# Gated attention and SwiGLU on one core: where the setup work, one chunk's input loads, the pair loads and several side streams are put in the order of the program

## The chip, the core and the metric

The kernel runs on one core of one Trainium2 chip. Its engines are TensorE (PE for matmuls, PEld for weight loads), VectorE (DVE), ScalarE (ACT), GpSimd (POOL) and SyncE (SP); transfers are issued by SP, ACT or POOL and run on the core's 16 DMA engines. The metric is the device time of one execution in microseconds, as the median of the runs; less is better. Times of instructions come from one execution that the hardware profiler recorded.

## What is computed

A sequence of 2048 rows of 640 numbers (`x`) goes through two branches, and a gate per row mixes them:

```python
def _A_ref(x, wq, wk, wv, wo, beta):        # 32 heads of 20, 4 chunks of 512 rows
    q, k, v = ...                            # x @ wq, x @ wk, x @ wv, by heads and chunks
    phi = lambda t: jnp.where(t > 0, t + 1.0, jnp.exp(t))
    g = _sigmoid(beta).reshape(1, H, 1, 1)
    for s in range(N):
        logits = jnp.einsum("bhqd,bhkd->bhqk", qs, ks) * scale + mask
        a_dot = jnp.einsum("bhqk,bhkd->bhqd", _softmax(logits), vs)
        num = jnp.einsum("bhld,bhde->bhle", phi(qs), M)
        den = jnp.einsum("bhld,bhd->bhl", phi(qs), z)[..., None] + 1e-6
        outs.append(g * num / den + (1.0 - g) * a_dot)
        M = M + jnp.einsum("bhld,bhle->bhde", phi(ks), vs)
        z = z + jnp.einsum("bhld->bhd", phi(ks))
    return o @ wo
...
g = _sigmoid((x * gate_w).sum(-1, keepdims=True))
a = _A_ref(x, wq, wk, wv, wo, beta)
b = (_silu(x @ w1) * (x @ w3)) @ w2
return g * a + (1 - g) * b
```

## The kernel before

**Number format.** Nearly every operand of a matmul is split into a high part of reduced precision and the rest (`split`, L204: ACT copies the high part, then DVE or POOL subtracts it), and a product takes three matmuls (`PASSES`: high by high, high by low, low by high).

**Halves.** Most matmuls use 64 of the 128 rows of the array, and the two row halves run side by side. A piece of dense work (`Work`) fills one PSUM bank: its first half is issued, then a no-op on SP that waits for the half's end (L308), and the second half waits for that no-op (L311). So SP's queue carries, beside the loads of weights and the stores, a no-op for each such piece.

**Two streams.** `attention()` (L1812) counts slots. Forty slots are a quad of four heads. In a quad `S_AT` and `T_AT` say at which slot the score matmuls (`s`), for the row maxima, and the transposed ones (`t`), which ACT turns into P by an exponential, are put into a queue; `PV` is the slot of the matmuls of P with V (`o`, line 1651). Two heads (a pair) lie in one of `NST` = 4 tiles `qk`, which `load_pair` (L1522) fills from memory by two DMAs on POOL's queue, at slots 28 and 39 of the quad before. A constant row of -1 stands in the tiles. Beside attention a list of segments (from L2024) brings the dense work: V, Q and K projections, the feed-forward products (`g`, `u` and, for chunks 0 and 1, the shared form `c1 w2 c6 c7 z5 c4 z3` of `ffn_pair`), the down projections (`f`), the reading and writing of the memory (`nd`, `pm`), the normalization (`rr`, `gt`) and the output projection (`op`). The head (L2038 and L2045) comes before attention begins; `LEAD` is the number of slots before the first quad.

**The planner.** The order of all instructions is written by the program itself. Each engine has a planned clock; `later` puts a step behind a planned time, `stages` chains evacuations, `go` adds a duration. `braid(a, b, every, skip)` yields the work of `a` and, each `every` ns of planned matmul time after the first `skip` ns, one step of `b`. Nothing of these times reaches the chip: there, an engine runs its instructions in the written order and waits for what they need. `AGE` (a weight load's least age), `SOON` (when a buffer of raw weights counts as free) and `AHEAD` (how far the second row half may run before the first when no bank is free) are such planned times.

**Around the change.** The setup has three parts: `constants` (L81, with the tile `one` that fills the -1 rows), `gates` (L93, five small DMAs of `beta` on POOL) and `selection` (L111, POOL work on three scratch tiles). Before the change `constants` is called behind the head's first job and `gates` and `selection` behind its second (L2080), ahead of the V tiles. `load_raw(2)` (L731) issues five DMAs of the third chunk's X on SP, all at once, into a buffer (`big_tile`) that the output projection of chunk 0 used before; in the program it stands behind that projection (L2054). `parts` (L813) evacuates a Q or K block through a tile of the ring `hT` (three tiles). `after_3` and `after_4` (L1408, L1419) are evacuations in `ffn_pair`.

Of the kernel before, what the change touches and what calls it, by code (L numbers as in the profile page):

```python
# [20 lines left out]
P = 128  # L21
# [10 lines left out]
RH, LEAD = 3 * DH, 23  # L32
NP, AGE, TS, PV = 2, 3000, 0, 2
LAG = 5
LATE = 4
EARLY = range(2, 6)
# [5 lines left out]
SOON = 700  # L42
COL, COL4, MIN_MM, APART, ISSUE, AHEAD = 0.4533, 1.7, 62, 5, 580, 1500
STEP, READ = 700, 222
EVAC = 3000
KSKIP, QSKIP = 6, 0
# [5 lines left out]
def gated_mix(ctx: ExitStack, tc: tile.TileContext, xT, wqk, wv, w13, w2, w2h, wo, beta, out):  # L52
# [28 lines left out]
    def constants():  # L81
        make_identity(nc, ident)
        nc.gpsimd.memset(mask, 0.0)
        nc.gpsimd.affine_select(mask[:, 384:], mask[:, 384:], pattern=[[-1, P]], base=0,
                                channel_multiplier=1, compare_op=ALU.is_ge, fill=BIG)
        for v in vg:
            nc.gpsimd.memset(v[:, :, VG:], 0.0)
        one = cp.tile([P, KB, L], F32, tag="oall", name="one", bufs=1)[:, 0]
        nc.gpsimd.memset(one, -1.0)
        for i in range(NST):  # L90
            nc.gpsimd.tensor_copy(qk[i][:, 1], one)

# [18 lines left out]
    def selection(base, h0, n, f0, f1):  # L111
# [16 lines left out]
        def done():  # L128
            for a in range(3):
                let(f"sel{base}_{a}")  # L130
            if not base:
# [5 lines left out]
               done=done)  # L137

# [592 lines left out]
    def load_raw(c):  # L731

        wide = big_tile(f"xr{c}")
        xraw[c] = [wide[:, kb * L:(kb + 1) * L] for kb in range(KB)]
        for kb in range(KB):
            store_later(xraw[c][kb], xT[c, :, kb, :], ("x", c, kb))
        return
        yield

    def new_x(c):  # L740

        got = []
        if c not in xraw:
            xraw[c] = []
# [68 lines left out]
    def parts(name, ps, bank, stored, phi=None, done=None, over=None):  # L813

        v = "dve" if over is None else "both"
        s = ht_tile([P, 2, L], FR, name)
# [507 lines left out]
    def ffn_pair(cs, plan, fill):  # L1324
# [4 lines left out]
        def block(j, idx):  # L1329
# [78 lines left out]
            def after_3(ps, bank):  # L1408
                t = H2[0][:, 0]
                stages(bank, ("dve", 690, lambda: nc.vector.tensor_add(ps, f["b"], ps)),  # L1410
                       ("dve", 690, lambda: nc.vector.tensor_mul(t, t, ps), True), done=lambda: end(0, "b"))
# [7 lines left out]
            def after_4(ps, bank):  # L1419
                t = H2[0][:, 1]  # L1420
                stages(bank, ("act", 600, lambda: nc.scalar.activation(t, ps, AF.Tanh, scale=0.5)),
# [390 lines left out]
    def attention():  # L1812


        for m in range(-1, NQUAD + 2):
            for n in range(40):
# [13 lines left out]
                if n in ((22, 32) if m < 0 else (28, 39)) and m + 1 < NQUAD:  # L1830
                    p = 2 * (m + 1) + (n > 28)
                    flush(lambda: all(q % NST != p % NST for _, _, q, _ in units))
                    load_pair(p)
# [200 lines left out]
    for n in range(9):  # L2034
# [10 lines left out]
    head += [braid(braid(chain([v0, v1, (0, islice(up[1], 2)), half, (0, islice(up[1], 15))]), (0, store_sums(A, True)), 1300), (0, load_sums(A)), 1200)]  # L2045
    seg = [braid(up, job_read(1), 4400, 14000)]
# [7 lines left out]
    seg = [braid(chain([d0, d1]), o1, 500, 6000), o2, (0, load_raw(2)), braid(chain([d1b, d2]), xs, 3000, 24400, False)]  # L2054
    seg += [braid(braid(chain([q2, v2]), out0, 900), xs, 1500, 5000)]
    ks = jobs_k_held(B)
    seg += ks[:KSKIP] + [alternate(chain(ks[KSKIP:]), job_plain(B, [0]))]
    segs.append((2 * H + 7, seg))
# [3 lines left out]
    seg += [braid(chain(q[:QSKIP] + [alternate(chain(q[QSKIP:]), job_plain(B, [1]))]), r, 2600, 3000, False)]  # L2062
# [4 lines left out]
    seg = [braid(braid(chain(main), chain([r, job_read(3)]), 1800, 7000), o1, 600, 1000),  # L2067
           braid(chain([o2, job_plain(B, range(4, 8))]), (0, store(1)), 900)]
    segs.append((3 * H + LAG + 5, seg))
    ups = [job_plain(B, range(8, 11)), job_half(3), job_half(2), job_plain(B, range(11, NF))]  # L2070
# [7 lines left out]
    tail = [braid(chain([d1b, d2]), o1, 300, 9000), o2]  # L2078

    def at_job(n):  # L2080
        if n == 0:
            constants()
        elif n == 1:
            gates()
            selection(0, 0, R1H + 1, 0, R1B * P)
# [92 lines left out]
```

## Time and profile before

| | |
|---|---|
| median of 3 runs | 1074.7 us (1073.06 to 1074.82) |
| profiled execution | 1080.68 us |
| its span, first to last instruction | 1079.0 us |
| mean granted clock of TensorE | 0.996 |
| memory traffic | 116.03 MB read, 70.25 MB written |

The span is what the page's lines share out; the profiled execution's own time lies 1.7 us above it. "PE L305" is a helper's line: nearly every dense matmul is issued there, so groups are told apart by the names of their tiles. A bracket in the timeline is the idle time of the engine just before a row, with what ended it.

### The profile page before, as it was taken

Reading aid. Unit: us, or ns where it says so; the run is one execution under the profiler, and the core shown is the slowest. Engines: PE = TensorE matmul, PEld = TensorE weight load, DVE = VectorE, ACT = ScalarE, POOL = GpSimd, SP = SyncE. Lnnn points to the kernel's source line nnn. Section 1 sums busy time; section 2 is a strip of 40 time slices with the busy share of each in tenths; the row PEclk is TensorE's granted clock in tenths of the full one; section 3 lists DMA queues with packets and bytes.
Section 4 is the critical chain, followed back from the end, with each engine's and each line's share of the span. In section 5 each row is a group of like instructions: output and inputs, shape, how many; then the busy total and the mean of one; then the engine's idle time right before and its main releaser. Section 6 shows DMA issues by size and latency. Waiting matters only on the chain.

```text
span 1079.0 us, 29746 instructions
## 1 busy us (share of the span) xinstructions
PE 1059.0 (98%) x11477; PEld 947.7 (88%) x11477; DVE 668.9 (62%) x1892; ACT 534.3 (50%) x1098; POOL 506.8 (47%) x740
## 2 busy tenths in 40 slices
PE   8999999999999999999999999999999999999998
PEld 6999988888889999899887887898788888999998
DVE  7556777777776676565454576765456666554552
ACT  6357565555554654465654544543434443664320
POOL 5213565655644462448454535545645544443230
PEclk9999999999999999999999999999999999999999
DMA  9655765454465755657686859554746455553631
GB/s 312 212 186 200 249 214 154 130 153 126 126 168 138 222 158 145 201 134 239 200 275 199 231 182 294 160 161 131 211 114 182 122 144 144 143 157 116 213 119 50
DMA packets 127109, 189.20 MB, mean 175 GB/s; under 512 B 21196, under 2 KB 65144, under 8 KB 126968
## 3 DMA queue, kind: packets, MB, share of 16 engines
q1 hardware_dynamic: 95928, 132.74, 39.6%
q0 software_dynamic: 23264, 40.40, 15.6%
q10 hardware_dynamic: 7776, 14.16, 3.7%
q8 instruction: 91, 1.49, 0.6%
q14 instruction: 50, 0.41, 0.1%
HBM read 116.03 MB, written 70.25 MB: 173 GB/s over the span
## 4 chain that ended last, share of the span: by engine, by line
PE 91%; DMA 4%; issue 1%; ACT 1%; POOL 1%; DVE 1%; SPq 0%; ACTq 0%; DVEq 0%; POOLq 0%
PE f L305 18%; PE c L305 11%; PE g L305 9%; PE u L305 7%; PE o L1651 7%; PE op L305 7%; PE v L305 6%; PE z L305 5%; PE s L1556 4%; PE t L1618 4%; PE k L305 3%; PE w L305 3%; PE q L305 3%; DMA qk<-qkd 2%; PE pm L305 1%; PE nd L305 1%
## 5 line engine op out<-in xcount | busy, mean ns | idle before, releaser
L1567 DVE CUSTOM_DVE_ANT_0 junk<-s,mask 128x128 bf16<-128x128 f32 (+3 forms) x512 | 251.0, 490 | 132.9 <-PE s L1556 91.3
L209 POOL TENSOR_TENSOR W<-wr,W 128x640 fp32r<-128x640 f32 (+2 forms) x112 | 175.4, 1572 | 149.1 <-ACT W L214 134.0
L1625 ACT ACTIVATE P<-t 128x384 f32<-128x384 f32 (+1 forms) x384 | 181.0, 526 | 126.6 <-PE t L1618 111.2
L305 PE MATMUL g<-X,W 64*128 64x512 f32 x900 | 217.1, 395 | 1.8 <-SPq L308 1.8
L305 PE MATMUL u<-X,W 64*128 64x512 f32 x780 | 191.8, 394 | 0.0
L1634 POOL TENSOR_SCALAR_AFFINE_SELECT P<-P 128x256 f32<-128x256 f32 (+1 forms) x192 | 96.2, 510 | 201.5 <-ACT P L1625 167.8
L214 ACT CAST W<-wr 128x640 fp32r<-128x640 f32 (+2 forms) x189 | 133.8, 720 | 57.9 <-PE f L305 32.5
L305 PE MATMUL f<-XW,W 64*128 64x320 f32 x1536 | 158.9, 310 | 2.6 <-SPq L308 2.6
L305 PEld LDWEIGHTS g<-X,W 64*128 64x128 f32 x900 | 149.0, 185 | 11.0 <-SPq L308 2.7
L305 PEld LDWEIGHTS f<-XW,W 64*128 64x128 f32 x1536 | 151.6, 187 | 4.1 <-SPq L308 3.1
L305 PE MATMUL c<-X,W 64*128 64x512 f32 x612 | 146.7, 396 | 0.1
L305 PE MATMUL f<-W,W 64*128 64x320 f32 x1056 | 137.4, 309 | 0.0
L305 PEld LDWEIGHTS u<-X,W 64*128 64x128 f32 x780 | 130.7, 185 | 5.9 <-issue 0.6
L305 PEld LDWEIGHTS f<-W,W 64*128 64x128 f32 x1056 | 116.3, 186 | 1.1 <-issue 0.8
L305 PE MATMUL c<-S,W 64*128 64x512 f32 x408 | 115.9, 395 | 0.0
L305 PE MATMUL op<-W,oT 64*128 64x320 f32 x960 | 103.7, 307 | 0.0
L305 PEld LDWEIGHTS c<-X,W 64*128 64x128 f32 x612 | 97.8, 185 | 6.2 <-ACT d L1358 0.6
L1577 POOL DMA_DIRECT2D qk<-mr x128 | 73.0, 572 | 63.0 <-DVE mr L1593 55.6
L1556 PE MATMUL s<-qk 60*128 60x256 f32 (+2 forms) x512 | 96.6, 329 | 3.5 <-DMA qk<-qkd 3.4
L305 PEld LDWEIGHTS op<-W,oT 64*128 64x128 f32 x960 | 98.6, 185 | 0.7 <-issue 0.6
L1618 PE MATMUL t<-qk 62*128 62x256 f32 (+2 forms) x512 | 93.7, 327 | 2.7 <-ACT P L1625 1.2
L305 PE MATMUL v<-W,X 64*128 64x320 f32 (+2 forms) x948 | 92.6, 310 | 0.0
(194 smaller groups left out, 2132.5 us busy)
## 6 DMA issues: line engine op xcount, KB each, us to landing
qk<-qkd POOLq DMA_DIRECT2D x128, 240.0 KB, 4.4
wr<-in_w_dram SPq DMA_DIRECT2D x82, 320.0 KB
hd<-H SPq DMA_DIRECT2D x26, 512.0 KB
qkd<-qs SPq DMA_DIRECT2D x20, 512.0 KB
qkd<-ks SPq DMA_DIRECT2D x20, 512.0 KB
wr<-hd SPq DMA_DIRECT2D x32, 320.0 KB
od<-oq ACTq DMA_DIRECT2D x32, 256.0 KB
wr<-in_wo_dram SPq DMA_DIRECT2D x20, 320.0 KB
```

What stands on the lines that cost most here:

```text
L209: return lambda: e.tensor_sub(dst[:, 1], src, dst[:, 0].bitcast(F32))
L214: stages(bank, ("act", ns, lambda: nc.scalar.copy(dst[:, 0], src)), low, done=done)
L305: ins = nc.tensor.matmul(o, l, x, start=not w.more and i == 0 and (r == 0 or not w.todo[0]), stop=i == len(todo) - 1 and (r == 1 or not w. ...
L1556: nc.tensor.matmul(ps[i][:, o:o + n], q[:, qb * P:(qb + 1) * P], k[:, :n], start=qb != 1, stop=qb != 0, skip_group_check=True)
L1567: nc.vector.tensor_tensor_reduce(out=junk[:, :n], in0=ps[i][:, o:o + n], in1=mask[:, L - n:], scale=1.0, scalar=-3.0e38, op0=ALU.add, op1= ...
L1577: nc.gpsimd.dma_start(dst, src)
L1618: nc.tensor.matmul(ps[i][:, o:o + L - q0], k[:, kb * P:(kb + 1) * P], q[:, q0:], start=kb != 2, stop=kb != 3, skip_group_check=True)
L1625: nc.scalar.activation(u["P"][:, i, o:o + n], ps[i][:, b:b + n], AF.Exp, scale=SCALE)
L1634: nc.gpsimd.affine_select(d, d, pattern=[[0, 2], [0, n], [1, P]], base=0, channel_multiplier=-1, compare_op=ALU.is_ge, fill=0.0)
L1651: nc.tensor.matmul(ps[32 * i:32 * i + 32, kb * P:], heads[2 * p + i]["v"][:, kb], pairs[p + i // 2]["P"][:, i % 2, o:o + n], start=kb == 0 ...
```

## The change

- `one` becomes a scratch tile; it fills only three of the four `qk` tiles at once. The new `set_up` calls `gates` and `selection` and fills the fourth tile's row 9000 ns of planned time later. The head calls it behind the first two V tiles (`islice(v0[1], 2)`); `at_job` keeps `constants` alone.
- The Q block `qs1_1` is evacuated through that fourth `qk` tile and not through the ring `hT`.
- `load_raw(2)` waits until the output projection of chunk 0 is planned as done and then yields after each of its five loads; it is a side stream of the down projection (`braid(..., (0, load_raw(2)), 1200, 0)`). `new_x` waits for it.
- The first pair load of a quad is at slot 27 in place of 28. `PV`, `LEAD`, `AGE`, `SOON`, `AHEAD` and `KSKIP` change.
- In `after_4` (`SOFT` holds 2, not 1) the bank is read once less: the multiply by `f["d"]` comes last, from memory to memory, on DVE or POOL. The new branch in `after_3` isn't taken.
- The steps of eight side streams and the ends of two segments change, and one plain tile goes from one segment to the one before.

```diff
-RH, LEAD = 3 * DH, 23
-NP, AGE, TS, PV = 2, 3000, 0, 2
+RH, LEAD = 3 * DH, 22
+NP, AGE, TS, PV = 2, 2500, 0, 3
+SOFT = (0, 2)
-SOON = 700
-COL, COL4, MIN_MM, APART, ISSUE, AHEAD = 0.4533, 1.7, 62, 5, 580, 1500
+SOON = 400
+COL, COL4, MIN_MM, APART, ISSUE, AHEAD = 0.4533, 1.7, 62, 5, 580, 3000
-KSKIP, QSKIP = 6, 0
+KSKIP, QSKIP = 4, 0
...
-        one = cp.tile([P, KB, L], F32, tag="oall", name="one", bufs=1)[:, 0]
+        one = f_tile("one", "pool")
         nc.gpsimd.memset(one, -1.0)
-        for i in range(NST):
+        for i in range(NST - 1):
             nc.gpsimd.tensor_copy(qk[i][:, 1], one)
+        big["one"] = one
...
+    def set_up():
+        gates()
+        selection(0, 0, R1H + 1, 0, R1B * P)
+        def fill():
+            nc.gpsimd.tensor_copy(qk[NST - 1][:, 1], big.pop("one"))
+            let("one", go("pool", 640))
+        later(now() + 9000, fill)
+        return
+        yield
...
     def load_raw(c):
+        while not all((c - 2, qb) in op_done for qb in range(4)):
+            yield 1
         wide = big_tile(f"xr{c}")
         xraw[c] = [wide[:, kb * L:(kb + 1) * L] for kb in range(KB)]
         for kb in range(KB):
             store_later(xraw[c][kb], xT[c, :, kb, :], ("x", c, kb))
-        return
-        yield
+            yield 1
     def new_x(c):
         got = []
+        while c == B[0] and c not in xraw:
+            yield 1
...
-        s = ht_tile([P, 2, L], FR, name)
+        if name == "qs1_1":
+            s = qk[NST - 1]
+            holds[name] = [0.0], 0
+        else:
+            s = ht_tile([P, 2, L], FR, name)
...
             def after_4(ps, bank):
                 t = H2[0][:, 1]
+                if 2 in SOFT:
+                    stages(bank, ("act", 600, lambda: nc.scalar.activation(t, ps, AF.Tanh, scale=0.5)),
+                           ("dve", 690, lambda: nc.vector.scalar_tensor_tensor(t, t, 1.0, ps, op0=ALU.add, op1=ALU.mult), True),
+                           either(690, 1290, lambda v: v.tensor_mul(t, t, f["d"])), done=lambda: end(1, "d"))
+                    return
...
-                if n in ((22, 32) if m < 0 else (28, 39)) and m + 1 < NQUAD:
-                    p = 2 * (m + 1) + (n > 28)
+                if n in ((22, 32) if m < 0 else (27, 39)) and m + 1 < NQUAD:
+                    p = 2 * (m + 1) + (n > 30)
...
-    head += [braid(braid(chain([v0, v1, (0, islice(up[1], 2)), half, (0, islice(up[1], 15))]), (0, store_sums(A, True)), 1300), (0, load_sums(A)), 1200)]
-    seg = [braid(up, job_read(1), 4400, 14000)]
+    head += [braid(braid(chain([(0, islice(v0[1], 2)), (0, set_up()), v0, v1, (0, islice(up[1], 2)), half, (0, islice(up[1], 15))]), (0, store_sums(A, True)), 1300), (0, load_sums(A)), 1800)]
+    seg = [braid(up, job_read(1), 3500, 14000)]
...
-    seg = [braid(chain([d0, d1]), o1, 500, 6000), o2, (0, load_raw(2)), braid(chain([d1b, d2]), xs, 3000, 24400, False)]
-    seg += [braid(braid(chain([q2, v2]), out0, 900), xs, 1500, 5000)]
+    seg = [braid(chain([d0, d1]), o1, 300, 7000), o2, braid(braid(chain([d1b, d2]), (0, load_raw(2)), 1200, 0), xs, 2700, 25400, False)]
+    seg += [braid(braid(chain([q2, v2]), out0, 300), xs, 1500, 3000)]
...
-    segs.append((2 * H + 7, seg))
+    segs.append((2 * H + 6, seg))
...
-    seg += [braid(chain(q[:QSKIP] + [alternate(chain(q[QSKIP:]), job_plain(B, [1]))]), r, 2600, 3000, False)]
+    seg += [braid(chain(q[:QSKIP] + [alternate(chain(q[QSKIP:]), job_plain(B, [1]))]), r, 2300, 0, False)]
...
-    seg = [braid(braid(chain(main), chain([r, job_read(3)]), 1800, 7000), o1, 600, 1000),
-           braid(chain([o2, job_plain(B, range(4, 8))]), (0, store(1)), 900)]
-    segs.append((3 * H + LAG + 5, seg))
-    ups = [job_plain(B, range(8, 11)), job_half(3), job_half(2), job_plain(B, range(11, NF))]
+    seg = [braid(braid(chain(main), chain([r, job_read(3)]), 900, 8000), o1, 1200, 8000),
+           braid(chain([o2, job_plain(B, range(4, 9))]), (0, store(1)), 1200)]
+    segs.append((3 * H + LAG + 6, seg))
+    ups = [job_plain(B, range(9, 11)), job_half(3), job_half(2), job_plain(B, range(11, NF))]
...
-    tail = [braid(chain([d1b, d2]), o1, 300, 9000), o2]
+    tail = [braid(chain([d1b, d2]), o1, 2700, 12000), o2]
...
     def at_job(n):
         if n == 0:
             constants()
-        elif n == 1:
-            gates()
-            selection(0, 0, R1H + 1, 0, R1B * P)
```

More of the change, by code (lines that the diff above doesn't have):

```diff
@@ L1409, in after_3 @@
                 t = H2[0][:, 0]
+                if 1 in SOFT:
+                    u = f["b"]
+                    stages(bank, ("dve", 690, lambda: nc.vector.tensor_add(u, u, ps), True),
+                           either(690, 1290, lambda v: v.tensor_mul(t, t, u)), done=lambda: end(0, "b"))
+                    return
                 stages(bank, ("dve", 690, lambda: nc.vector.tensor_add(ps, f["b"], ps)),
@@ L1420, in after_4 @@
                 t = H2[0][:, 1]
+                if 2 in SOFT:
+                    stages(bank, ("act", 600, lambda: nc.scalar.activation(t, ps, AF.Tanh, scale=0.5)),
+                           ("dve", 690, lambda: nc.vector.scalar_tensor_tensor(t, t, 1.0, ps, op0=ALU.add, op1=ALU.mult), True),
+                           either(690, 1290, lambda v: v.tensor_mul(t, t, f["d"])), done=lambda: end(1, "d"))
+                    return
                 stages(bank, ("act", 600, lambda: nc.scalar.activation(t, ps, AF.Tanh, scale=0.5)),
```

## The prediction

> **What bounds the kernel now.** I read the page's first part, then the chain, then every piece of PE idle time in order of time.
>
> ```profile
> span 1079.0 us, 29746 instructions
> PE 1059.0 (98%) x11477; PEld 947.7 (88%) x11477; DVE 668.9 (62%) x1892; ACT 534.3 (50%) x1098; POOL 506.8 (47%) x740
> PE 91%; DMA 4%; issue 1%; ACT 1%; POOL 1%; DVE 1%; SPq 0%; ACTq 0%; DVEq 0%; POOLq 0%
> ```
>
> PE is busy for 98% of the span and 91% of the chain. The edits leave the matmuls as they are; they move other instructions against them. So the change is worth what it does to the places where PE stops. The timeline of PE shows them as idle time in brackets; these are all the pieces over 0.15 us between its first and last matmul:
>
> ```profile
> 12.35 11.61 PE L904 MATMUL q<-X,W 128*128 128x512 f32 x42 [2.27 <-ACT X L689]
> ...
> 138.91 0.35 PE L1556 MATMUL s<-qk 60*128 60x256 f32 x1 [0.69 <-DMA qk<-qkd]
> 139.94 0.47 PE L1556 MATMUL s<-qk 60*128 60x256 f32 x3 [0.67 <-DMA qk<-qkd]
> ...
> 435.04 0.89 PE L305 MATMUL f<-XW,W 64*128 64x320 f32 x7 [2.57 <-SPq L308]
> ...
> 516.52 0.47 PE L1618 MATMUL t<-qk 62*128 62x256 f32 x3 [0.45 <-DVE m L1567]
> 569.38 0.50 PE L305 MATMUL g<-X,W 64*128 64x512 f32 x1 [1.47 <-SPq L308]
> 610.64 0.50 PE L305 MATMUL g<-X,W 64*128 64x512 f32 x1 [0.37 <-SPq L308]
> ...
> 661.86 0.24 PE L303 MATMUL gt<-ident,gm 64*128 64x64 f32 x1 [1.53 <-DMA gm<-gd]
> 674.24 0.49 PE L1618 MATMUL t<-qk 62*128 62x512 f32 x1 [0.97 <-ACT gate L993]
> 679.10 0.50 PE L1618 MATMUL t<-qk 62*128 62x256 f32 x3 [1.18 <-ACT P L1625]
> ...
> 775.62 0.47 PE L1556 MATMUL s<-qk 60*128 60x256 f32 x3 [0.90 <-DMA qk<-qkd]
> 799.85 0.39 PE L1556 MATMUL s<-qk 60*128 60x256 f32 x2 [0.72 <-DMA qk<-qkd]
> 874.36 0.47 PE L1556 MATMUL s<-qk 60*128 60x256 f32 x3 [0.46 <-DMA qk<-qkd]
> ```
>
> They sum to 14.25 us; the first and the one at 435 make 4.84 of it, the other eleven 9.41. Two cost more than they last. The view by windows gives the granted clock in its third column from the end:
>
> ```profile
> 12.40:15.90 3.50, 3.50 (x9) 2.73 (x10) 3.38 (x6) 3.18 (x6) 0.00 (x0) 0.51 1.05 395
> 426.00:432.00 6.00, 6.00 (x83) 5.99 (x81) 3.41 (x10) 1.79 (x4) 2.09 (x4) 1.00 0.33 85
> 432.50:435.00 2.50, 0.00 (x0) 0.00 (x0) 2.50 (x5) 0.96 (x4) 0.00 (x0) 1.00 0.61 187
> 435.00:439.20 4.20, 4.16 (x34) 4.16 (x36) 0.20 (x1) 1.48 (x3) 0.00 (x0) 0.59 0.94 304
> ```
>
> After the gap of 2.27 us the clock stands at 0.51 for 3.5 us, after that of 2.57 us at 0.59 for 4.2 us: 3.5 x 0.49 = 1.7 us and 4.2 x 0.41 = 1.7 us are lost on top. (34 matmuls in 4.2 us against 83 in 6.0 us say the same.) After the gaps of 1.47 and 1.53 us I see no such stretch. So what can be won is 14.25 + 3.4 = 17.7 us at most.
>
> **The change, part by part.**
>
> *The third chunk's X by pieces (saves 4.2).* SP's rows before the gap at 435:
>
> ```profile
> 432.36 1.28 SPq L802 DMA_DIRECT2D xr<-in_xT_dram  x3
> ...
> 434.32 1.09 SPq L802 DMA_DIRECT2D xr<-in_xT_dram  x2
> ```
>
> SP works through its instructions one behind the other, as the rows show. The five loads write the buffer that the output projection of chunk 0 reads until about 432, and only then can they issue. Behind them stands the no-op of line 308, for which the second row half of an f tile waits, and PE with it. After the change a load is issued only when all four blocks of that projection are planned as done, and one per 1200 ns of planned matmul time, so each holds SP for some 0.4 us (1.28 / 3) and its no-ops pass between. Nothing needs the pieces soon: the splits begin 25400 ns of matmul time into the stage. Gone: 2.57 + 1.7 = 4.3; I leave 0.1 for five short holds. Bounds: 0 (a piece waits as the five did) to 4.3.
>
> *Gates and selection behind V tiles (saves 2.5).*
>
> ```profile
> 4.76 0.91 SPq L684 DMA_DIRECT2D xr<-in_xT_dram  x2
> 5.38 0.73 POOL L94 DMA_DIRECT2D gH<-in_beta_dram  x1
> 6.10 2.09 POOL L96 DMA_DIRECT2D cR<-in_beta_dram  x4
> 11.68 1.14 ACT L689 CAST X<-xr 128x512 fp32r<-128x512 f32 x2 [3.28 <-DMA xr<-in_xT_dram]
> 19.88 0.38 POOL L965 MEMSET V<- 128x128 f32 x1 [10.50 <-DVE W L209]
> q0 software_dynamic: 76, 0.02, 20.3%
> ```
>
> The last X pieces are issued at 4.76 and are waited for until 11.68. Between, POOL issues five small loads; the last row is the DMA view of 8.0 to 11.7, where POOL's queue takes 20.3% of the engines, 0.203 x 3.7 = 0.75 us of each, for 0.02 MB. The five now stand behind the V tile's memset on POOL, at 19.9 or later, when PE has V tiles to work on and no gap before 138; selection follows them on POOL, ends some 3 us later than now, and its first reader is far off. If X comes 0.75 sooner, the gap is 1.5 us, as long as those that leave the clock alone: 0.8 + 1.7 = 2.5. Bounds: 0 (other traffic delays X) to 2.27 + 1.7 = 4.0 (X beats the last matmul at 10.1).
>
> By the Trainium skill ("DMA: Bandwidth & Descriptors", Queues, rings and completion order) each DMA engine serves its queue rows in turn, a packet at a time. By that rule the small loads share engines with X though another queue issues them, and the term is not nothing; by issue order alone it would be 0.
>
> *Pair loads a slot sooner (saves 1.6).*
>
> ```profile
> 767.83 1.58 POOL L209 TENSOR_TENSOR W<-wr,W 128x640 fp32r<-128x640 f32 x1 [2.72 <-ACT W L214]
> 769.34 1.11 POOL L1531 DMA_DIRECT2D qk<-qkd  x2
> POOL qk L1531 <- PE t L1618: 5.9, 4, 4.7
> 777.00 2.29 PE o L1651 x32
> 900.38 2.29 PE o L1651 x32
> ```
>
> Five quads (o to o) take 123.4 us, a slot of 40 therefore 0.62 us. The five gaps of s on qk<-qkd total 3.44; at 138 the two belong to one pair. Moved by 0.62 they save 4 x 0.62, less 0.16 because the last is only 0.46: 2.3. But a weight split of 1.58 us stands right ahead of the load, and the load keeps that place if the split isn't passed. I take 1.6; bounds 0 and 3.44. Sooner also means that POOL may wait for the t matmuls that still read the buffer (5.9 us in four waits now, 0.62 more in each), with masks queued behind; P masks have one slot more (PV 3), so I cost that at nothing here and in the new waits below.
>
> *Reads and output tiles of chunk 1 re-paced (saves 1.8).*
>
> ```profile
> 653.88 0.81 POOL L1744 DMA_DIRECT2D gm<-gd  x1
> 655.00:660.00 5.00, 5.00 (x69) 4.54 (x59) 3.48 (x8) 2.61 (x5) 3.26 (x5) 1.00 1.05 354
> 565.88 2.59 SPq L802 DMA_DIRECT2D qkd<-ks  x2
> ```
>
> The gaps at 661, 673 and 678 (3.68 together) lie where gm is fetched while the DMA engines are full (1.05 of their time). The memory read now starts 3000 ns sooner and steps by 2300 in place of 2600, the normalization begins at 8000 in place of 1000 and steps by 1200 in place of 600, which leaves each fetch twice the time. Half of 3.68: 1.8; bounds 0 and 3.68.
>
> *K and Q stages (saves 0.4).* The gaps at 516, 569 and 610 sum to 2.29. The long one follows 2.59 us in which SP waits to store a K block; KSKIP 4 moves the plain tiles two K blocks forward, so the meeting is another one, better or worse. Bounds -2.29 and 2.29.
>
> *Edits that I cost at nothing.*
>
> ```profile
> L1422 DVE TENSOR_TENSOR c<-d,c x13: 686/693/697, 158.7 to 351.6; 128x512 f32<-128x512 f32 x13
> L303 PE MATMUL gt<-ident,gm x40: 213/222/224, 1026.6 to 1034.3; 64*128 64x64 f32 x40
> 1057.05 17.88 PE L305 MATMUL op<-W,oT 64*128 64x320 f32 x217
> ```
>
> SOFT frees a bank one DVE multiply (693 ns, 13 times) sooner and may send the multiply to POOL; between 140 and 432 PE has no gap, so nothing is won. The Q block in attention's tile and the -1 rows filled later lie under the dense V tiles. In the tail the steps of the last normalization grow from 300 to 2700 ns: ten tiles from about 1021 end near 1021 + 27 = 1048, and the projection starts at 1057; 9 us of cover. Were it gone, PE would wait by the difference.
>
> *New waits (cost 4.3).* SOON, AGE, AHEAD, segment ends and steps shift nearly every queue from 430 to 900. There the trace shows no such order, so I bound it: 0 new waits, or as many as the eleven now, 9.4. A mean of 9.41 / 11 = 0.86; I take five, 4.3, the middle.
>
> **Sum.** 4.2 + 2.5 + 1.6 + 1.8 + 0.4 = 10.5 saved, 4.3 spent: 6.2. The profiled execution took 1080.68 us (span 1079.0 and 1.7 around it), so 1074.5; it is 6.0 above the median of 1074.7. The gaps are absolute, so I take 6.2 from the median: **1068.5 us**. Its own range: the gates' term by its bounds moves it by -1.5 to +2.5, the new waits, taken halfway to their bounds, by -2.2 to +2.5: 1064.8 to 1073.5. Chance 0.56.
>
> **Rivals.**
> - *All goes to its upper end.* 4.2 + 4.0 + 2.3 + 3.7 + 2.3 = 16.5, less 4.3: 12.2, 1062.5. For it: each wait has its edit. Against: POOL's order. 0.12.
> - *Gaps come back elsewhere.* As many new waits as the eleven, 9.4: 10.5 - 9.4 = 1.1, 1073.6. For it: nearly all lie within 2 us, the size by which edits move things. 0.10.
> - *The load isn't spread.* If the planner runs ahead of the chip, the first piece still waits for its buffer: 6.2 - 4.2 = 2.0, 1072.7. Against: SP would have to reach it before the f tile behind the projection. 0.06.
> - *SP blocks PE more (slower).* With SOON 400 a weight load is issued 300 ns sooner after a split that POOL or DVE may not have ended; SP then stands before its no-ops as at 432. A stop like that costs 2.57 + 1.7 = 4.3. The place is the f and g tiles from 430 on. Two of them give 8.6 - 6.2 = +2.4, 1077.1; from the second on it decides. Against: SP's stops reach PE only three times now. 0.12.
> - *The clock isn't lost to gaps of this size.* If the half clock came from elsewhere, 1.7 + 1.7 fall out: 6.2 - 3.4 = 2.8, 1071.9. The two stretches begin right after the two longest gaps, which speaks against it. 0.04. The Trainium skill ("TensorE: Matmul & The Clock Gate", HAM oscillation) gives as the abstract rule that idle gaps over about 3.4 us are to be avoided; by it 2.57 would be harmless, and this trace disagrees with its 0.59.
>
> **Chances.** A measurement tells about 0.2%, 2.1 us, from no change. Of the forecast's 0.56 the end above 1072.6 (0.04) counts as no change. Faster: 0.52 + 0.12 + 0.04 = 0.68. Same: 0.10 + 0.06 + 0.04 = 0.20. Slower: 0.12. The range runs from 1061.5, a microsecond past the best case, to 1077.2, two stops of SP.
>
> **What would show it.** Right: no gap and full clock near 435; the first gap at most 1.5 us and the clock not at half after 12; gaps of s under 0.3; none at 660 to 680. Wrong: L308 ahead of new gaps of 2 us or more, or idle PE before 1057 in the tail. New gaps of together over 10.5 us would turn the sign.

## The result and the profile after

| | before | after |
|---|---|---|
| median | 1074.7 us (1073.06 to 1077.22, 5 runs) | 1062.61 us (1061.73 to 1063.17, 5 runs) |
| ratio of the times, 95% interval | | 0.9885 [0.987, 0.99] |
| profiled execution, its span | 1080.68 us, 1079.0 us | 1063.17 us, 1061.5 us |
| mean granted clock | 0.996 | 1.000 |

The change saves 12.1 us; 6.2 were forecast. The first lines of the page after:

```profile
span 1061.5 us, 29740 instructions
PE 1051.9 (99%) x11477; PEld 939.8 (89%) x11477; DVE 672.4 (63%) x1903; ACT 533.3 (50%) x1098; POOL 499.9 (47%) x729
```

The matmuls are the same 11477. PE's time without work, span less busy time, fell from 20.0 to 9.6 us. The timeline of PE after the change, all pieces of idle time over 0.15 us between its first and last matmul (start, duration, operation, in brackets the idle time just before it and what ended it):

```profile
28.25 2.03 PE L320 MATMUL v<-W,X 64*128 64x320 f32 x24 [0.30 <-SPq L323]
...
129.95 0.39 PE L320 MATMUL pm<-V,pkn 64*128 64x147 f32 x1 [0.71 <-ACT pkn L1060]
...
155.08 0.34 PE L320 MATMUL nd<-Ms,pq 64*128 64x84 f32 x1 [1.02 <-ACT P L1657]
...
160.88 0.50 PE L320 MATMUL w<-X,W 64*128 64x512 f32 x1 [0.31 <-SPq L323]
...
232.06 0.50 PE L320 MATMUL c<-X,W 64*128 64x512 f32 x1 [0.34 <-ACT d L1380]
...
433.26 1.00 PE L320 MATMUL f<-XW,W 64*128 64x320 f32 x10 [0.35 <-SPq L323]
...
688.17 0.44 PE L1650 MATMUL t<-qk 62*128 62x384 f32 x1 [0.57 <-ACT P L1657]
...
799.08 0.49 PE L320 MATMUL g<-X,W 64*128 64x512 f32 x1 [0.95 <-SPq L323]
```

Eight pieces, 4.55 us, in place of thirteen, 14.25 us. Only the place at 433 had a gap before, and there 0.35 is left of 2.57. No row is ended by a DMA any more, where before s on qk<-qkd and gt on gm<-gd were. The windows of after that answer to those shown of before:

```profile
12.00:15.90 3.90, 3.90 (x19) 3.13 (x18) 3.90 (x7) 3.75 (x8) 0.00 (x0) 1.00 1.04 403
429.00:433.00 4.00, 3.90 (x53) 3.64 (x49) 3.19 (x10) 3.09 (x8) 0.58 (x2) 1.00 0.79 254
433.00:437.00 4.00, 3.74 (x52) 3.74 (x54) 2.39 (x4) 1.46 (x2) 3.99 (x8) 1.00 0.98 329
640.00:675.00 35.00, 35.00 (x480) 31.67 (x476) 24.58 (x80) 15.93 (x37) 17.22 (x31) 1.00 0.85 263
```

The clock (third column from the end) is full in all of them; the down projection behind the third chunk's loads issues 52 matmuls in 4 us where it issued 34 in 4.2. Between 640 and 675 PE never stops.

How the two profiled executions differ: 14.25 - 4.55 = 9.7 us of such gaps and twice 1.7 us of half clock make 13.1 of the 17.5 us between the spans. Of the other 4.4, 0.7 is idle time in shorter pieces (10.4 - 9.7), and 3.7 lies in PE's busy time (1059.0 - 1051.9 = 7.1, less 3.4), where no row shows a wait. A rough count finds the greater part of it: PE counts as busy, too, where one row half works and the other stands. With each matmul counted from its start for 0.4533 ns per column (the planner's `COL`; twice that at half clock), matmuls of one row half alone run for 96.7 and 96.9 us in two traces of before (the second is that of the first experiment below) and for 91.4 and 92.6 us in two of after. The level hangs on the cost per column, the difference hardly. One half alone does half the work, so the 4.3 to 5.3 us less are worth an estimated 2.2 to 2.7 us. Such time shows in no bracket. What makes the rest was not found.

Two stages as they stand now. The head, timeline of POOL and of ACT and the DMA view of 8.0 to 11.7:

```profile
17.89 0.74 POOL L96 DMA_DIRECT2D gH<-in_beta_dram  x1
```

```profile
9.15 0.63 ACT L704 CAST X<-xr 128x512 fp32r<-128x512 f32 x1 [0.86 <-DMA xr<-in_xT_dram]
10.26 0.62 ACT L704 CAST X<-xr 128x512 fp32r<-128x512 f32 x1 [0.48 <-DMA xr<-in_xT_dram]
```

```profile
q1 hardware_dynamic: 632, 1.15, 97.1%
```

The loads of beta left for 17.89 and later; in the window POOL's queue has no row any more, the hardware queue takes 97.1% of the engines, and the last two splits of X begin at 9.15 and 10.26, not both at 11.68. PE doesn't stop in the head. SP's rows about 430:

```profile
430.44 2.23 SPq L820 DMA_DIRECT2D xr<-in_xT_dram  x2
...
433.27 0.36 SPq L820 DMA_DIRECT2D xr<-in_xT_dram  x1
434.95 0.33 SPq L820 DMA_DIRECT2D xr<-in_xT_dram  x1
```

The first two pieces still hold SP for 2.23 us, the first 0.43 and the second 1.76. By the trace the buffer was free: the last matmul of the projection that read it ended at 427.9, 2.5 us before the first piece. Why the second takes so long isn't shown. The later ones take 0.36 and 0.33, and the f tile waits 0.35 for its no-op.

### The profile page after: what moved, and what is told of

Read it like the earlier page. It is cut to its first block, busy times and chain, and to the rows that moved or that the text cites. A ratio compares the mean times of both kernels' runs of the same rounds, so it can differ in the third digit from the quotient of the medians.

```text
span 1061.5 us, 29740 instructions
## 1 busy us (share of the span) xinstructions
PE 1051.9 (99%) x11477; PEld 939.8 (89%) x11477; DVE 672.4 (63%) x1903; ACT 533.3 (50%) x1098; POOL 499.9 (47%) x729
## 4 chain that ended last, share of the span: by engine, by line
PE 93%; DMA 3%; DVE 2%; ACT 1%; SPq 1%; issue 1%; DVEq 0%
PE f L320 18%; PE c L320 11%; PE g L320 10%; PE u L320 7%; PE o L1683 7%; PE op L320 7%; PE v L320 6%; PE z L320 5%; PE t L1650 4%; PE s L1588 4%; PE q L320 4%; PE k L320 3%; PE w L320 3%; PE pm L320 1%; PE nd L320 1%; DVE junk L1599 1%
## 5 line engine op out<-in xcount | busy, mean ns | idle before, releaser
L320 PE MATMUL f<-XW,W 64*128 64x320 f32 x1536 | 156.2, 308 | 0.4 <-SPq L323 0.4
L320 PEld LDWEIGHTS g<-X,W 64*128 64x128 f32 x900 | 146.8, 185 | 11.0 <-issue 1.4
L320 PEld LDWEIGHTS f<-XW,W 64*128 64x128 f32 x1536 | 148.2, 185 | 1.8 <-SPq L323 0.9
L320 PE MATMUL v<-W,X 64*128 64x322 f32 (+2 forms) x948 | 92.4, 310 | 0.3 <-SPq L323 0.3
L1650 PE MATMUL t<-qk 62*128 62x256 f32 (+2 forms) x512 | 91.4, 326 | 0.6 <-ACT P L1657 0.6
L1588 PE MATMUL s<-qk 60*128 60x256 f32 (+2 forms) x512 | 90.2, 326 | 0.0
```

Source lines behind the costliest of these rows:

```text
L320: ins = nc.tensor.matmul(o, l, x, start=not w.more and i == 0 and (r == 0 or not w.todo[0]), stop=i == len(todo) - 1 and (r == 1 or not w. ...
L1588: nc.tensor.matmul(ps[i][:, o:o + n], q[:, qb * P:(qb + 1) * P], k[:, :n], start=qb != 1, stop=qb != 0, skip_group_check=True)
L1650: nc.tensor.matmul(ps[i][:, o:o + L - q0], k[:, kb * P:(kb + 1) * P], q[:, q0:], start=kb != 2, stop=kb != 3, skip_group_check=True)
```

## The experiments

All were timed against the kernel before on the same chip. "Alone" means the kernel before with one edit; "taken back" means the changed kernel without one. Line numbers differ by kernel. A ratio's interval reaches 0.0011 to 0.002 to each side, 1.2 to 2.1 us; what an edit taken back costs is the difference of two ratios times 1074 us, so it is good to 2 or 3 us. The first theory was that each gap belongs to one edit, as the prediction's terms have it; the rival, that the gaps belong to the whole written order, and that an edit elsewhere moves them.

### The kernel before, once more

> The kernel before once more, for a second trace of it. Theory 1 (every gap of PE is written into the order of the program): the same 13 gaps to within 0.3 us each, in sum 13 to 15.5 us, with half clock after 12 and after 435, and an execution of 1080 us. Rival (gaps whose end is a transfer differ from one execution to the next; the profiled execution was 6.0 above the median because some of them were long in it): the gap at 435 stays at 2.4 to 2.8 because no transfer ends it, but the first gap and those at 661 to 678 come out 0.5 us or more shorter in an execution near 1075.

One execution: 1076.65 us, span 1074.9. Its timeline of PE, the pieces up to 680 but for one of 0.45 at 516:

```profile
11.07 1.67 PE L904 MATMUL q<-X,W 128*128 128x512 f32 x6 [0.66 <-ACT X L689]
...
12.97 0.49 PE L904 MATMUL q<-X,W 128*128 128x512 f32 x1 [0.23 <-ACT X L689]
...
13.70 1.66 PE L904 MATMUL q<-X,W 128*128 128x512 f32 x6 [0.23 <-DVE X L692]
...
137.43 0.35 PE L1556 MATMUL s<-qk 60*128 60x256 f32 x1 [0.77 <-DMA qk<-qkd]
138.46 0.47 PE L1556 MATMUL s<-qk 60*128 60x256 f32 x3 [0.68 <-DMA qk<-qkd]
...
435.16 0.85 PE L305 MATMUL f<-XW,W 64*128 64x320 f32 x7 [2.57 <-SPq L308]
...
670.61 0.50 PE L1618 MATMUL t<-qk 62*128 62x512 f32 x1 [0.99 <-ACT gate L993]
675.48 0.50 PE L1618 MATMUL t<-qk 62*128 62x256 f32 x3 [1.18 <-ACT P L1625]
```

And two of its windows:

```profile
139.40:142.80 3.40, 3.40 (x19) 3.40 (x18) 2.34 (x8) 2.63 (x5) 1.97 (x5) 0.51 0.63 151
435.20:438.60 3.40, 3.40 (x32) 3.40 (x34) 0.12 (x1) 1.48 (x3) 0.00 (x0) 0.68 0.99 308
```

The order is the same, the gaps are not. The gap of 2.57 at 435 and the two of t by 670 to 680 stand as they were. The first gap is 0.66 with two of 0.23 behind it, not 2.27, and the clock stays full there. The gaps of 1.47 at 569, 0.37 at 610 and 1.53 at 661 are absent. The two of s at 138, 0.77 and 0.68, are followed by half clock, which the same two of 0.69 and 0.67 in the first trace are not. So the gaps that end when a transfer lands come, go or change their length with the execution; those at 435, 516, 670 and 675, which work of a queue or an engine ended, came both times. Those at 569 and 610 came once, although no transfer ended them: SP's no-op did, behind stores for which SP waited on DVE (a K block `ks` at 569, `rs` and `ns` at 610). So the kind of releaser alone doesn't tell. Four terms of the prediction rested in part on rows of the first kind: the beta loads, the pair loads, the reads of gm, and the K and Q stages.

### The beta loads alone behind two V tiles

```diff
         elif n == 1:
-            gates()
             selection(0, 0, R1H + 1, 0, R1B * P)
...
-chain([v0, v1, (0, islice(up[1], 2)), half
+chain([(0, islice(v0[1], 2)), (0, set_up()), v0, v1, (0, islice(up[1], 2)), half
```

Here `set_up` holds `gates` alone.

> Before, with the five loads of beta moved behind the first two V tiles and nothing else. Theory 1 (they hold up the last X pieces on the DMA engines): the first gap falls from 2.27 us to under 0.5, no half clock after 12, V begins 2.5 to 3.6 us sooner and the time falls by 2.5 to 3.5 us (ratio 0.997 to 0.998). Rival (X is late by itself): the gap stays above 1.5 us and the time within 1 us of before.

1072.05 us (11 runs) against 1073.65: ratio 0.9985 [0.9974, 0.9996], 1.6 us saved. The ACT row, the DMA view of 8.0 to 11.7, and PE's gap at 431:

```profile
9.24 1.28 ACT L695 CAST X<-xr 128x512 fp32r<-128x512 f32 x2 [0.75 <-DMA xr<-in_xT_dram]
```

```profile
q1 hardware_dynamic: 689, 1.26, 99.5%
```

```profile
430.99 0.90 PE L311 MATMUL f<-XW,W 64*128 64x320 f32 x7 [2.58 <-SPq L314]
```

The head has no gap and the splits start at 9.24: five loads of 0.02 MB together did hold X back. The gap of 2.58 stays, as it should. The term is real and smaller than the 2.5 forecast and the 2.5 to 3.5 expected here. One reason in sight is that the first gap is mostly shorter than the 2.27 of the trace that I read: 0.66 in the second one, and 1.13 and 0.92 in the next two runs, which leave the head as it was.

### The third chunk's X by pieces alone

```diff
+        while not all((c - 2, qb) in op_done for qb in range(4)):
+            yield 1
...
             store_later(xraw[c][kb], xT[c, :, kb, :], ("x", c, kb))
-        return
-        yield
+            yield 1
...
-o2, (0, load_raw(2)), braid(chain([d1b, d2]), xs, 3000, 24400, False)]
+o2, braid(braid(chain([d1b, d2]), (0, load_raw(2)), 1200, 0), xs, 3000, 24400, False)]
```

> Before, with the third chunk's X loaded by pieces as a side stream of the down projection and nothing else. Theory 1: the gap at 435 falls from 2.57 us to under 0.5, no half clock there, the time falls by 3.5 to 4.3 us (ratio 0.996 to 0.997). Rival (the first pieces still meet a buffer in use, SP stands before its no-ops): a gap of 1 us or more stays at 430 to 440 and the time falls by less than 2 us.

1069.23 us (5 runs): ratio 0.9965 [0.9953, 0.9978], 3.8 us saved. SP's rows, and two windows:

```profile
429.28 0.33 SPq L805 DMA_DIRECT2D xr<-in_xT_dram  x1
...
433.63 0.35 SPq L805 DMA_DIRECT2D xr<-in_xT_dram  x1
434.50 1.67 SPq L805 DMA_DIRECT2D xr<-in_xT_dram  x2
```

```profile
432.00:435.00 3.00, 3.00 (x46) 3.00 (x44) 2.58 (x8) 1.09 (x3) 1.29 (x3) 1.00 0.78 238
435.00:439.20 4.20, 4.20 (x60) 2.66 (x58) 2.66 (x10) 0.58 (x2) 3.05 (x6) 1.00 1.05 318
```

Where PE stood still it issues 46 matmuls, and 60 where it issued 34 at a clock of 0.59. The step is right in mechanism and size: 3.8 measured, 4.2 forecast.

### The new pacing of chunk 1 alone

```diff
-alternate(chain(q[QSKIP:]), job_plain(B, [1]))]), r, 2600, 3000, False)]
+alternate(chain(q[QSKIP:]), job_plain(B, [1]))]), r, 2300, 0, False)]
...
-chain([r, job_read(3)]), 1800, 7000), o1, 600, 1000)
+chain([r, job_read(3)]), 900, 8000), o1, 1200, 8000)
```

> Before, with the new steps of the memory reads and of the normalization of chunk 1 (2300/0, 900/8000, 1200/8000) and nothing else. Theory 1: the three gaps at 661, 673 and 678 (3.68 us) go, and stops of one row half beside them too: the lead at equal matmul work grows by 4 to 6.5 us between 640 and 690, the time falls by 3 to 6 us (ratio 0.994 to 0.997). Rival (most of the lead there is from the moved K and Q stages and the other edits before it): the lead grows by less than 2 us and the time falls by less than 2 us.

1076.85 us (10 runs): ratio 1.0029 [1.0016, 1.0042], 3.1 us **slower**. Its timeline of PE:

```profile
667.32 1.58 PE L305 MATMUL v<-W,X 64*128 64x320 f32 x17 [0.90 <-ACT gate L993]
...
697.87 0.44 PE L1618 MATMUL t<-qk 62*128 62x384 f32 x1 [1.05 <-ACT P L1625]
...
1002.75 1.14 PE L305 MATMUL f<-XW,W 64*128 64x320 f32 x12 [1.01 <-SPq L308]
```

The wait on gate is still there, another tile now; the wait on P has moved to 698, and a new one of 1.01 stands at 1003, far behind the edit. For the edit by itself the term has the wrong sign, and both expectations missed. The gaps of this trace total 8.5 us, those of the second trace of before 9.5: they don't account for the loss, and where it lies was not found.

### Gates and selection taken back to the head

```diff
     def set_up():
-        gates()
-        selection(0, 0, R1H + 1, 0, R1B * P)
...
             constants()
+        elif n == 1:
+            gates()
+            selection(0, 0, R1H + 1, 0, R1B * P)
```

> The changed kernel with gates and selection called behind the head's second job again, as before the change. Theory 1 (a part is worth the same in either kernel; the five loads alone gave 0.9985): the first gap is back, 0.5 to 2.5 us and other from run to run, the time is 1064 to 1066 us (ratio 0.990 to 0.9915). Rival (in the changed kernel the head has other slack): 1062 to 1063 us, as the changed kernel.

1070.73 us (11 runs): ratio 0.9977 [0.9966, 0.9988]; against 0.9885 of the whole change that costs 9.9 us. The head's gap and the window behind it:

```profile
12.48 2.92 PE L923 MATMUL q<-X,W 128*128 128x512 f32 x6 [2.39 <-ACT X L701]
```

```profile
12.50:15.90 3.40, 3.40 (x8) 2.72 (x9) 3.29 (x5) 3.05 (x5) 0.00 (x0) 0.50 1.04 401
```

The head loses 2.39 + 1.7 = 4.1 us of the 9.9. From 132 on ten gaps of 0.29 to 1.11 us total 6.8, where the whole change has seven of together 4.25; none of the ten is ended by work of the setup. That leaves some 3 us of the loss without a gap. Both expected times were too low.

### The five loads at once again

```diff
-        while not all((c - 2, qb) in op_done for qb in range(4)):
-            yield 1
...
-            yield 1
+        return
+        yield
...
-o2, braid(braid(chain([d1b, d2]), (0, load_raw(2)), 1200, 0), xs, 2700, 25400, False)]
+o2, (0, load_raw(2)), braid(chain([d1b, d2]), xs, 2700, 25400, False)]
```

> The changed kernel with the five loads of the third chunk's X issued at once again. Theory 1 (pieces alone gave 0.9965): the gap of 2.5 us with half clock behind it is back near 430 and the time is 1066 to 1067 us (ratio 0.992 to 0.993). Rival (the two pieces that still hold SP for 2.2 us in the changed kernel do nearly the same harm): less than 2 us are lost, 1063 to 1064.5 us.

1063.49 us (5 runs): ratio 0.992 [0.9907, 0.9933], 3.8 us above the whole change. PE's gap, SP's row and the window behind the gap:

```profile
427.92 1.30 PE L320 MATMUL f<-XW,W 64*128 64x320 f32 x13 [1.75 <-SPq L323]
```

```profile
426.05 2.23 SPq L819 DMA_DIRECT2D xr<-in_xT_dram  x5
```

```profile
429.00:432.50 3.50, 3.50 (x52) 3.50 (x50) 2.00 (x7) 1.17 (x3) 0.00 (x0) 1.00 0.98 313
```

The gap is back, 1.75 long, and the window behind it has full clock. The trace is that of the fastest of five runs (1062.56 to 1066.7). The ratio is that of theory 1, the median time lies in the rival's range; at 2 or 3 us to each side the two aren't told apart. So the edit's worth in company agrees with its 3.8 alone, but only as far as that.

### The pair loads at slot 28 again

```diff
-else (27, 39)) and m + 1 < NQUAD:
+else (28, 39)) and m + 1 < NQUAD:
```

> The changed kernel with the first pair load of a quad at slot 28 again. Theory 1 (the slot alone is what removed the gaps of s on qk<-qkd): such gaps come back, 0.3 to 1 us each at three or more places, in sum 1.5 to 3.5 us, and with two near each other sometimes half clock; the time is 1064 to 1066.5 us (ratio 0.990 to 0.9925). Rival (POOL's order around the loads, set by the other edits, is what matters): none or one such gap, the time within 1 us of the changed kernel's 1062.6.

1061.52 us (4 runs): ratio 0.9896 [0.9882, 0.9909]; the interval overlaps that of the whole change, and no cost is seen. The waits of PE in the second trace of before (waiting line, releaser: us, times, longest) begin with

```profile
PE s L1556 <- DMA qk<-qkd: 3.2, 6, 0.8
```

and neither the whole change nor this kernel has such a row at all. So it isn't the slot that keeps the waits of s away in this company. Alone, on the kernel before, the slot was not timed.

### The old pacing of chunk 1 in the changed kernel

```diff
-r, 2300, 0, False)]
+r, 2600, 3000, False)]
...
-chain([r, job_read(3)]), 900, 8000), o1, 1200, 8000)
+chain([r, job_read(3)]), 1800, 7000), o1, 600, 1000)
```

> The changed kernel with the steps of the memory reads and of the normalization of chunk 1 as before (2600/3000, 1800/7000, 600/1000). Theory 1 (the new steps remove the stops at 640 to 690, in the company of the other edits, though alone they gave 1.0029): gaps and one-sided stops are back there, 3 us or more, the time is 1065.5 to 1069 us (ratio 0.991 to 0.995). Rival (the stops there went with the moved K and Q stages; the new steps are worth nothing or cost): the time is 1060 to 1063 us.

1065.64 us (5 runs): ratio 0.9929 [0.9916, 0.9941], 4.7 us above the whole change. The edit that alone costs 3.1 us saves 4.7 in this company: its worth is not its own. Theory 1 has the time right, but its gaps don't show: the trace, that of the fastest run (1063.57), has no gap of PE over 0.15 us between 231 and 798. What shows is one row half that stands. Timeline of PE:

```profile
686.34 2.80 PE L320 MATMUL u<-X,W 64*128 64x512 f32 x11
```

Eleven matmuls of 64 rows follow one another here, mostly 0.23 us apart, and no other matmul starts between them, though PE is busy without a break. Where both halves run, two start in that time (w and c at 297, in the trace of the run with the planned times taken back). By the count of the section on the result, matmuls of one half alone run for 11.5 us between 660 and 700, against 6.3 and 6.7 in the two traces of the whole change.

### Gates and selection moved together, on the kernel before

```diff
-        elif n == 1:
-            gates()
-            selection(0, 0, R1H + 1, 0, R1B * P)
...
+        gates()
+        selection(0, 0, R1H + 1, 0, R1B * P)
```

The second pair of lines is the body of the `set_up` called as in the first edit.

> Before, with gates and selection both moved behind the first two V tiles (no other edit). The five loads alone gave 0.9985 with the order of all else unchanged; selection takes planned POOL time, so moving it changes which engine the planner gives later weight splits to, and with them the order of about one POOL instruction in six. Theory 1 (the order around the moved selection is what frees the stretches from 100 to 560 us): 1064 to 1068 us (ratio 0.991 to 0.995). Rival 1 (only the head's loads count): 1071 to 1073 us (ratio 0.998 to 0.999). Rival 2 (a changed order without the other edits brings new waits): slower than 0.9985 by 2 us or more.

1076.82 us (12 runs) against 1073.67: ratio 1.0034 [1.0016, 1.0053], 3.6 us **slower**, 5.3 worse than the beta loads alone, which is selection's part. Timeline of PE and a window:

```profile
129.07 0.49 PE L1563 MATMUL s<-qk 60*128 60x512 f32 x1 [1.18 <-DVE m L1574]
130.38 0.37 PE L310 MATMUL pkt<-ident,pk 64*128 64x64 f32 x1 [0.59 <-DVE qs L832]
...
183.64 0.49 PE L312 MATMUL c<-X,W 64*128 64x512 f32 x1 [1.27 <-ACT d L1365]
```

```profile
130.40:133.80 3.40, 3.40 (x22) 2.75 (x24) 3.22 (x10) 0.38 (x2) 0.00 (x0) 0.56 1.04 373
```

This is rival 2. Selection is POOL work of the head, and with its move PE waits at 129 and 184 for DVE and ACT, which are far from the head. The way that this goes is the planner: with POOL's plan changed, 19 instructions move from POOL to DVE (740 and 1892 instructions before, 721 and 1911 here). Which of them makes which wait isn't shown.

### Selection alone taken back

```diff
     def set_up():
         gates()
-        selection(0, 0, R1H + 1, 0, R1B * P)
...
+        elif n == 1:
+            selection(0, 0, R1H + 1, 0, R1B * P)
```

> The changed kernel with selection alone called behind the head's second job again; the five loads stay late. Putting both back cost about 9 us, 3.7 of it before 25 us in the one execution traced. Theory 1 (that loss has two parts: the loads' hold on X, 1.5 to 3.7 us, and the order that selection's place gives, 5 us): the head is as in the changed kernel and the loss is 4 to 7 us spread over 100 to 560 us (ratio 0.992 to 0.9955). Rival (all of it is the loads): within 1 us of the changed kernel.

1067.65 us (6 runs): ratio 0.9937 [0.9918, 0.9957], 5.6 us above the whole change, with an intact head. Timeline of PE:

```profile
128.99 0.50 PE L1587 MATMUL s<-qk 60*128 60x512 f32 x1 [1.17 <-DVE m L1598]
```

As theory 1 has it. The gap is of the same kind and at the same tile as in the run before it, by the opposite edit. Beside the run with both taken back (0.9977) it gives the beta loads' hold in this company: 0.0040, 4.3 us, as the head's 4.1 there says.

### The planned times taken back

```diff
-NP, AGE, TS, PV = 2, 2500, 0, 3
+NP, AGE, TS, PV = 2, 3000, 0, 2
-SOFT = (0, 2)
+SOFT = (0,)
-SOON = 400
+SOON = 700
-... APART, ISSUE, AHEAD = ... 580, 3000
+... APART, ISSUE, AHEAD = ... 580, 1500
```

> The changed kernel with AGE 3000, SOON 700, AHEAD 1500, PV 2 and without the branch of SOFT, as before. Theory 1 (these move queues by less than the waits there and are worth nothing in themselves, but the other steps were set in their company): 1063 to 1068 us (ratio 0.989 to 0.994), with new gaps and no one of them over 1.5 us. Rival (SP's earlier loads harm PE): without them the gap of g on the no-op at 798 goes and the time is 1 us or more under the changed kernel's.

1070.16 us (11 runs): ratio 0.9965 [0.9953, 0.9978], 8.6 us above the whole change. Timeline of PE and a window:

```profile
663.40 0.50 PE L1650 MATMUL t<-qk 62*128 62x512 f32 x1 [1.74 <-ACT gate L1015]
689.28 0.50 PE L1588 MATMUL s<-qk 60*128 60x512 f32 x2 [1.29 <-ACT P L1657]
```

```profile
663.40:666.80 3.40, 3.40 (x32) 3.40 (x33) 0.57 (x3) 1.51 (x3) 1.55 (x3) 0.62 0.46 126
```

I had costed these edits at nothing, or counted them among the new waits. Without them the wait on gate is 1.74 and takes 1.7 of half clock with it: 3.4 of the 8.6. About 3.3 more are lost between 260 and 300, where the trace has no idle row over 0.15 us. About half of that is one row half that stands: between 260 and 310 matmuls of one half alone run for 4.3 us, against 1.2 in both traces of the whole change, an estimated 1.5 us. A window there:

```profile
299.60:301.50 1.90, 1.90 (x12) 1.35 (x10) 1.76 (x6) 1.37 (x3) 0.00 (x0) 1.00 0.32 108
```

PE is busy throughout at full clock, but issues 12 matmuls in 1.9 us, where the 4 us from 295 to 299 have 38. The rest was not found. The five values were put back together; which of them does it isn't shown. Theory 1's time was too low, and so was its bound for a gap; the rival fell as well, since the gap of g is still there, 0.73 at 805.

### The changed kernel, once more

> The changed kernel once more, for a second trace and beside the others on one chip. Theory 1 (its gaps are of the order, not of transfers): the same eight gaps to within 0.3 us and a spread of the times under 2 us, against 5 to 6 us of before; ratio 0.987 to 0.990. Rival: gaps that come and go as in the two traces of before.

1061.71 us (6 runs, 1060.93 to 1063.17): ratio 0.9884 [0.9864, 0.9904]. Its trace has gaps of 0.70, 1.01, 0.17, 0.33, 0.20, 0.46 and 0.86, and six of the seven stand at places of the first trace, each within 0.15 us of its length there; the pieces of 0.30 at v and 0.35 at f are absent. The gaps of this kernel are those of its order. Its times lie within 2.2 us of each other, where the 21 runs of before in the first comparison span 6.1 (1071.54 to 1077.67); in the result, with five runs each, it is 1.4 against 4.2. That fits a kernel with no gap left that a transfer ends, but the spread wasn't traced to that.

One more reading of these two second traces: I summed the matmuls' cost in order (columns by 0.46 ns, half of it for 64 rows or fewer; 1086 us in all) and compared the times at which both kernels reach the same share of work. The changed kernel is ahead by 3.7 us at 100 us of work (the head, and some 2 us without a gap), 7.1 at 140 (the pair loads with their half clock), 5.8 at 400, 9.9 at 440 (the third chunk's X), 12.5 at 640, 14.8 at 680 (the waits on gate and P of chunk 1), and 14.3 at the end. Where the orders differ this is good to a microsecond or two. So the gain comes in steps, the larger ones where gaps and half clock went; but the 2.6 us between 440 and 640 come where before has a single gap, of 0.45.

## Why the prediction was half right

**What held.** The sign, and that most of the gain lies in PE's gaps and the clock behind them: 13.1 of 17.5 us between the profiled executions. **X by pieces**: 4.2 forecast, 3.8 alone, 3.8 taken back. **The beta loads**: that they hold X back, with a size near or inside its bounds of 0 to 4.0 (2.5 forecast, 1.6 alone, 4.3 in the changed kernel's company); but the last two splits of X began 2.4 us sooner without them (9.24 for 11.68), not the 0.75 that I took from their share of the engines. **New waits**: 4.3 forecast, and after the change the gaps total 4.55. That is luck: I looked for them between 430 and 900, where they total 1.87; the other 2.68 stand before 240. **The tail**: costed at nothing, and PE has no gap behind 799. **SP's stops** did not grow: waits ended by SP total 1.9 us in the changed trace, four of them, the longest 0.95, so the slower rival fell. Of the rival that the load isn't spread one half was seen: the first two pieces held SP for 2.23 us, at a price of 0.35; its reason was not, since the projection had ended 2.5 us before.

**Which step failed.** The sum of gains. Of 17.7 us that could be won I let the edits take 10.5, because I gave each gap to the edit nearest to it and then took half or less: 1.6 of 3.44, 1.8 of 3.68, 0.4 of 2.29. In fact every old gap went, but for 0.35 at 433: 14.25 + 3.4 - 4.55 = 13.1 between the two profiled executions. The measured 1062.61 lies outside the forecast's own range, 1064.8 to 1073.5; it is the time of the rival in which all goes to the upper end, 1062.5. Its reason, though, that each wait has its edit, fell with the runs; that the numbers meet is luck too. The upper limit of 17.7 had a hole as well: it counts only time in which PE stands as a whole, and 3.7 of the 17.5 us between the profiled executions lie in PE's busy time, in good part where one row half stood.

- *Pair loads a slot sooner*, 1.6: taken back, about nothing. The waits of s stay away with either slot, so something else of the change removed them; what, isn't shown.
- *Re-paced reads*, 1.8: alone 3.1 slower, in company 4.7 faster.
- *Selection*: I wrote that its first reader is far off and stopped there. Its move costs 5.3 us on the kernel before and saves 5.6 in the company of the other edits; the planner sets later work in another order with it.
- *Edits costed at nothing*: AGE, SOON, AHEAD, PV and SOFT are together worth 8.6 us in company. I had bounded SOFT by the instruction that it moves (693 ns of DVE where PE has no gap) and counted SOON, AGE and AHEAD among the new waits, as a cost. "PE has no gap there, so nothing is won" doesn't follow: taken back, they cost some 3.3 us between 260 and 300 without a gap.
- *K and Q stages*, 0.4: their gaps are gone, but two of the three were absent from the second trace of before as well. This was not tried alone.

Taken back one at a time, the edits cost 9.9 + 3.8 + 1.2 + 4.7 + 8.6 = 28 us, of a change that is worth 12. Two edits have a worth of their own, 3.8 + 1.6 = 5.4 us. The other 7 are not the sum of parts that can be priced one by one: of the edits timed alone, the pacing cost time and so did selection beside the beta loads, and both save time in company. The planned times, the pair loads, the K and Q stages, `LEAD` and the ends of the segments were not timed alone. The runs don't show which queue's order removes which wait, nor why just this combination fits; that stays open.

**The baseline.** I took all gaps of one trace as the kernel's own. Those that a transfer ended were partly that execution's, which was 6 us above the median. By the second trace not 17.7 but 9.5 + 3.4 = 12.9 us could be won in this way. The error made the terms too large and the halving made them too small, so it doesn't show in the sum.

**The clock.** "The gaps of 1.47 and 1.53 leave the clock alone" was true of that trace and wrong as a rule of length: 1.45 us in two pieces halved it in the second trace, and 1.75 in one piece did not where the five loads went at once. The last section has a better measure.

## What to carry to other kernels

Where a program plans its own order, separate the edits that remove a wait in a queue (a load that stands before no-ops and isn't free to issue; small loads beside urgent ones) from those that shift planned times: the first could be priced from a trace here, to a microsecond or two; the second had no price of their own, and are to be timed together. Take two traces of the kernel before pricing a gap: here what a transfer ended came and went, and four that an engine's or a queue's work ended stayed. Count for a gap the clock behind it, which here cost 1.7 us each time that it was halved. And where two halves of an engine run side by side, look for the time in which one of them stands: no bracket shows it.

## What the runs showed of the hardware

**The clock is decided by windows, not by the length of a gap.** In the clock records of the fourteen traces of this case, half clock begins ten times before the kernel's end, lasts 3.413 us each time, and begins in each execution on one grid of 3.413 us that runs from the first change of the clock. I cut each trace by its grid and added up the time in each cell in which no matmul runs. All ten half clocks follow a cell with at least 1.39 us of it: 2.27 and 2.57 in the first trace of before, 1.45 and 2.16 in the second, 2.39, 2.49, 2.58, 1.74, and 1.39 and 2.57 in the run with gates and selection moved. No cell under 1.35 is followed by one. Two others, of 1.35 and 1.55, were left alone. So in these traces the bound lies at about 1.4 us of 3.4, and not sharply: 1.39 and 1.45 halved the clock, 1.55 did not (the run with the five loads at once), and why isn't shown. Short gaps add up when they fall into one cell (0.77 + 0.68), and a gap across a border counts in parts: those of 1.47 and 1.53 in the first trace of before put at most 0.92 into one cell. There, too, a border falls into the first of the two gaps of s, 0.69 and 0.67, and the clock stayed full behind them. The changed kernel's fullest cell has 1.02. The Trainium skill ("TensorE: Matmul & The Clock Gate", Part 1: The HAM clock gate) says that the chip watches a free-running window of activity, about 3.4 us long; the grid of these traces agrees.

**Small loads can hold large ones back.** The DMA view of 8.0 to 11.7 in the second trace of before:

```profile
q0 software_dynamic: 47, 0.02, 26.8%
q1 hardware_dynamic: 333, 0.61, 59.6%
```

On POOL's queue 0.02 MB take 26.8% of all engines for 3.7 us (20.3% in the first trace), and the queue that brings X has 59.6%, 0.61 MB; without the five loads (the changed kernel, and the beta loads moved alone) it has 97.1% and 99.5%, 1.15 and 1.26 MB in the same time. Both queues together take 86% with the loads, so X lost more than the small loads' own share; by what, isn't shown.
